# A fused sketch-attention and MLP kernel: the same operations in another order on every engine and in other PSUM banks

## The chip, the cores and the metric

The kernel runs on one core of a Trainium2 chip. The metric is the device time of one execution in microseconds; three runs of the kernel before took 102.84, 103.22 and 104.95 us (median 103.22). A core has five engines that work side by side, each through its own queue in order: TensorE (PE, matrix products into PSUM), VectorE (DVE), ScalarE (ACT), GpSimd (POOL) and SyncE (SP). SP and ACT issue the transfers (DMA) here. An instruction waits until what it reads is written and what it overwrites has been read; whatever stands behind it on its engine waits too.

## What is computed

```python
# attention: q, k, v are (4 batches, 4 heads, 1088 rows, 32); S1, S2 are (8, 32), float64
phi(x): a = x @ S1.T; b = x @ S2.T; return outer(a, b) as 64 features per row
kv  = sum over rows of phi(k)^T v          # (64, 32) per head
z   = sum over rows of phi(k)              # (64,)
x   = (phi(q) @ kv) / (phi(q) @ z + 1e-6)  # heads side by side: (4, 1088, 128)
# block: g_ln (128), w_ch1 (128, 512), w_ch2 (512, 128), the weights float64
xn  = (x - mean) / sqrt(var + 1e-6) * g_ln
out = x + relu(xn @ w_ch1) @ w_ch2         # (4, 1088, 128), float32
```

## The kernel before

Nothing is left to a scheduler. The function defines small named operations (marked `@op`) and a string `PROGRAM` that lists them, with engine letters (`V` VectorE, `A` ScalarE, `G` GpSimd, `S` SyncE) and PSUM bank letters as arguments. The order of the string is the order on each engine's queue. There are eight PSUM banks, `A` to `D`, `M`, `N`, `O`, `K`. A later writer of a bank waits for the readers of what stood there.

The stages, which the string interleaves for the four batches 0 to 3:

- **Loads.** `ld_s`, `ld_g`, `ld_w`, `ld`, `ld_h`, `ld_v`, `ld_vr` fetch the sketches, g, the weights, k and q, and v; `ld_vr` fetches the two last row groups of v in short rows. Constants, masks and pads are made by the `c_` operations; `c_cg` folds g and the mean into a 128x128 matrix.
- **Weights.** The weights come as float64 bit patterns. Operations `w_ex`, `w_bits`, `w_exf`, `w_mant`, `w_low`, `w_e2`, `w_e3`, `w_add` and `w_mul` turn them into float32 by handling exponent, mantissa and low word; index 0 is the sketches, 1 is w_ch1, 2 is w_ch2. `fold` and `fold_cp` multiply w_ch1 by the matrix of `c_cg`.
- **Keys.** `turn_g` and `turn_r` turn k on VectorE; `k_feat` multiplies it by the sketch on PE (L506); `k_tok` turns the features back on VectorE (L516); `k_prod` makes the 64 products per row on GpSimd or VectorE (L82); `k_sum`, `k_zs`, `k_sc` and `k_sccp` make z and put it beside the sketch of q; `k_val` forms kv (L560); `k_vcp`, `k_spr`, `k_rcp` spread it.
- **Queries.** `turn_h`, `turn_r`, `q_feat` (L629), `q_tok` (L639), then `q_ac`, `q_den`, `q_rec` for the denominator, `q_a2` and `q_prod` for the products, `q_turn` (L677), and `num` (L735), which gives x turned, in banks A to D; `num_cp` and `num_r` copy it to SBUF. The first half of batch 0 takes a path of its own: `q_dir` (L595), `q_ac0`, `q_b0`, `q_prod0`, `q_flip`, `q_flcp` and `num0`; `v_flip` and `v_cp` turn v of batch 0 on PE.
- **Block.** x is cut into ten chunks: 0 to 7 of 512 rows, two per batch, and 8 and 9 of 128. `hid` is the first matmul (L843), `relu` its rectifier, `sec` the second matmul for 128 rows (L859). `row_pe`, or `row_turn`, `row_wr` and `row_rd` through DRAM, give x with rows on partitions for the statistics `st_bn`, `st_ag`, `st_pow`; `fin`, or `fin_a` and `fin_g`, scale and add; `store` and `store_r` write out.

`fill` and `bump` are matmuls of ones into bank M whose results nobody reads; they occupy PE where it would wait. The operation around the change that the program's order decides most is a matmul pair such as

```python
    @op
    def hid(z, c, j, t0, t1):
        a, n = P * t0, P * (t1 - t0)
        pe.matmul(banks[z][:, 0:n], w1[:, P * j : P * (j + 1)], cols(c)[:, a : a + n], start=True,
                  stop=True)
```

whose bank `z` must be free and whose columns `cols(c)` must have been copied.

## Time and profile before

| | us |
|---|---|
| profiled execution, its own time | 102.81 |
| its span in the trace | 100.9 |
| PE busy | 95.3 |
| DVE busy | 74.0 |
| POOL busy | 58.4 |
| ACT busy | 41.3 |

The profile is of one execution. The span runs from the first instruction to the last; 1.9 us of the time lie outside it. Busy shares are means over the span. Rows of a timeline start with the start and the length in us, then the engine, the line, the operation and what it writes and reads; a bracket gives idle time of that engine before it and what ended that idle time. Rows of the chain that ended last have start, length and the thing that the end waited for. A float32 matmul counts as two passes in the rows, so that "x2" is one matmul.

### The profile page before, as it was taken

To read this page: it belongs to the slowest core of one execution; us is meant where nothing else is said; L and a number is where in the kernel's file an instruction comes from. 1 tells how busy PE (TensorE), PEld (TensorE's weight loads), DVE (VectorE), ACT (ScalarE), POOL (GpSimd) and SP (SyncE) were. 2 spreads that over 40 slices of the span, in tenths; PEclk is the share of its full clock that TensorE was granted. 3 is DMA by queue.
4 is the path that set the end of the run, shared out by engine and by line. 5 is a ranking of instruction groups with operands and counts; after the bars stand their busy time and mean duration, and the time that the engine had idled before them with its cause. 6 is when DMAs were issued, how large, how long until landed. Compare 5 with 4: busy or idle time off the path is not lost.

```text
span 100.9 us, 3433 instructions
## 1 busy us (share of the span) xinstructions
PE 95.3 (94%) x1355; PEld 68.7 (68%) x1355; DVE 74.0 (73%) x239; ACT 41.3 (41%) x119; POOL 58.4 (58%) x83
## 2 busy tenths in 40 slices
PE   5988999999999999999999999999999999999960
...
PEclk9999999999999999999999999999999999999999
...
GB/s 76 272 293 389 353 370 275 272 218 88 3 6 301 212 164 3 6 130 0 6 107 106 47 59 0 109 153 187 55 107 204 143 122 148 1 115 132 77 119 64
DMA packets 12367, 13.85 MB, mean 137 GB/s; under 512 B 2880, under 2 KB 8768, under 8 KB 12352
## 3 DMA queue, kind: packets, MB, share of 16 engines
...
q14 instruction: 5, 0.04, 0.2%
...
## 4 chain that ended last, share of the span: by engine, by line
PE 78%; DMA 5%; POOL 5%; DVE 2%; ACT 2%; SPq 2%; issue 1%; ACTq 0%; POOLq 0%
PE bankO L859 8%; PE bankM L859 8%; DMA w_raw<-in_moe_w_ch_dram 5%; PE bankN L843 5%; PE bankK L560 5%; PE bankC L843 4%; PE bankK L843 4%; PE bankK L859 4%; PE bankB L843 3%; PE bankA L843 3%; PE bankD L843 3%; PE bankM L250 3%; PE bankA L859 3%; PE bankN L859 3%; POOL ob L888 2%; PE bankA L735 2%
## 5 line engine op out<-in xcount | busy, mean ns | idle before, releaser
L82 POOL TENSOR_TENSOR kp<-kf 128x1024 f32<-128x1024 f32 (+4 forms) x9 | 15.9, 1779 | 0.1
L827 POOL TENSOR_SCALAR va<-mv 128x4 f32<-128x4 f32 (+1 forms) x10 | 2.3, 228 | 18.2 <-DVE mv L822 17.7
L82 POOL TENSOR_TENSOR qp<-a,fq 128x1280 f32<-128x1280 f32 (+1 forms) x5 | 11.1, 2219 | 0.2
L859 PEld LDWEIGHTS bankO<-w,hT 128*128 128x128 f32 x80 | 9.7, 192 | 1.9 <-issue 1.9
L829 POOL TENSOR_TENSOR rstd<-va,mhalf 128x4 f32<-128x4 f32 (+1 forms) x10 | 10.3, 1034 | 0.8
L859 PE MATMUL bankO<-w,hT 128*128 128x128 f32 x80 | 10.4, 277 | 0.0
L859 PEld LDWEIGHTS bankM<-w,hT 128*128 128x128 f32 x72 | 9.0, 192 | 1.9 <-issue 1.9
L677 DVE STREAM_TRANSPOSE qpT<-qp 128x1280 f32<-128x1280 f32 (+1 forms) x7 | 9.6, 1365 | 0.0
L250 PE MATMUL bankM<-ones 128*128 128x256 f32 (+1 forms) x28 | 8.3, 440 | 1.2 <-DVE top L180 1.2
L859 PE MATMUL bankM<-w,hT 128*128 128x128 f32 x72 | 9.3, 275 | 0.0
L816 DVE BATCH_NORM_STATS2 st<-x 128x6 f32<-128x128 f32 x32 | 6.7, 272 | 2.5 <-issue 2.5
L250 PEld LDWEIGHTS bankM<-ones 128*128 128x128 f32 x28 | 5.7, 241 | 2.5 <-DVE top L180 1.2
L851 ACT ACTIVATE hT<-bankC 128x512 f32<-128x512 f32 (+1 forms) x6 | 3.3, 551 | 8.3 <-PE bankB L859 4.7
L843 PE MATMUL bankC<-xT,w 128*128 128x512 f32 x12 | 6.1, 592 | 0.0
L843 PE MATMUL bankN<-xT,w 128*128 128x512 f32 (+1 forms) x14 | 6.1, 516 | 0.0
L851 ACT ACTIVATE hT<-bankN 128x256 f32<-128x256 f32 (+1 forms) x6 | 3.0, 498 | 7.2 <-PE bankN L843 7.2
L82 POOL TENSOR_TENSOR a<-fq,rden 128x160 f32<-128x160 f32 (+1 forms) x6 | 2.8, 463 | 5.2 <-DVE rden L659 4.8
L560 PEld LDWEIGHTS bankK<-kp,vn 128*32 128x32 f32 x288 | 4.2, 110 | 2.3 <-issue 1.1
L851 ACT ACTIVATE hT<-bankK 128x512 f32<-128x512 f32 (+1 forms) x6 | 3.1, 522 | 6.2 <-PE bankK L843 5.3
L457 DVE STREAM_TRANSPOSE qT<-qn 128x512 f32<-128x512 f32 x8 | 5.5, 687 | 0.0
L843 PE MATMUL bankK<-xT,w 128*128 128x512 f32 (+1 forms) x12 | 5.4, 530 | 0.0
L735 PE MATMUL bankD<-qpT,kvr 32*32 32x288 f32 (+1 forms) x64 | 5.2, 386 | 0.0
...
## 6 DMA issues: line engine op xcount, KB each, us to landing
...
```

What stands on the lines that cost most here:

```text
L82: by[eng].tensor_tensor(out=o, in0=a, in1=b, op=ALU.mult)
L250: pe.matmul(M[0][:, 0:w], ones[:, 0:P], ones[:, 0:w], start=True, stop=True)
L457: dve.transpose(_ap(dst[b % 2], 0, P, P * 4 * half, [[32, 4], [P, 4], [1, 32]]), src[b][:, 512 * half : 512 * half + 512],)
L560: pe.matmul(KV[D * h : D * h + D, 0:F], vn[b][:, TW * h + D * u : TW * h + D * (u + 1)], kp[:, H * F * u + F * h : H * F * u + F * (h + 1) ...
L677: dve.transpose(_ap(qpT, 0, P, 32 * u0, [[32, u1 - u0], [TW, 8], [1, 32]]), qp[:, H * F * u0 : H * F * u1])
L735: pe.matmul(X[r][D * h : D * h + D, o : o + w], kvr[b % 2][rows, DM * f + D * h : DM * f + D * h + D], qpT[rows, c : c + w], start=(f == 0 ...
L816: dve.bn_stats(out=sts[slot(c)][:, 6 * t : 6 * t + 6], in_=row_ap(c, t))
L827: pool.tensor_scalar(out=vas[slot(c)][:, 0:n], in0=_ap(mvs[slot(c)], 0, P, 1, [[2, n]]), scalar1=1e-6, scalar2=None, op0=ALU.add)
L829: pool.tensor_tensor(out=rstds[slot(c)][:, 0:n], in0=vas[slot(c)][:, 0:n], in1=mhalf[:, 0:n], op=ALU.pow)
L843: pe.matmul(banks[z][:, 0:n], w1[:, P * j : P * (j + 1)], cols(c)[:, a : a + n], start=True, stop=True)
L851: act.activation(o, i, AF.Relu)
L859: pe.matmul(banks[z][:, DM * t : DM * (t + 1)], h[:, 512 * j + P * t : 512 * j + P * (t + 1)], w2[:, DM * j : DM * (j + 1)], start=(j == 0 ...
```

## The change

Only the string is changed. The same operations stand in another order, and many have another engine letter or another bank; the unused `sk_0` is left out. On loads: both sketches are loaded by ScalarE's queue (`ld_s A`), g by SyncE instead of ScalarE, and all `row_rd` and `row_wr` by SyncE; the short rows of v for batches 1 and 2 come earlier on SyncE, the rest of w_ch1 before k of batch 1. The words of the sketches are worked out on VectorE alone, ahead of the masks. The four turning products of v (`v_flip`) follow each other, in banks M, K, O and C. `fold D` comes after `k_val 0`, and `fold B` replaces `fold M`. The first half of w_ch1 is multiplied on VectorE (`w_mul V 1 0 256`). Of chunk 0 three `hid` come ahead of `q_feat 1`, three `sec` of chunk 0 come ahead of `num 0` and the four of chunk 1 together ahead of `num 1`. `k_val 2` comes just after `num 1`; `q_feat 3` and `k_val 3` come after chunk 3's `hid`, most of `sec 2` and half of `sec 3`.

The start and the part around batch 3's queries in the two strings:

```diff
-ld_w S 1 2 4; c_ones; ld_g A; c_small; c_ac 0; ld_s A 0; ld_s S 1; c_vpad 0; c_kvb; c_vpad 1;
-fill 1 128; ld S k 0 0 16; c_act; c_pads 1; c_pads 0; fill 4 256; c_iota; ld S k 0 16 34;
-c_ac 1; c_m2; c_ident; ld_w S 1 0 2; c_m32; c_m8; ld S k 1 0 34; ld S q 0 16 34;
-w_low A 1 256 512; w_ex V 0 0 32; w_bits V 0 0 32; w_bits V 1 256 512; w_exf A 0 0 32;
-ld_h S q 0 0; w_mant V 1 256 512; w_mant A 0 0 32; w_ex V 1 256 512; ld S v 0 0 32;
-w_e2 V 0 0 32; w_addlow V 0 0 32; w_exf A 1 256 512; w_e3 V 0 0 32; turn_g k 0 0 2;
-ld_vr S 0 1; s_heads G; fill 1 128; w_e2 A 1 256 512; fill 1 128; c_cg V; ld_vr S 0 0; bump 12;
-turn_g k 0 2 4; ld_w S 2 0 4; sk; bump 24; sk_8 A; w_e3 V 1 256 512; sk_q; turn_r k 0;
-ld S q 1 0 34; w_ex V 1 0 256; w_add V 1 256 512; k_feat 0 0 9; w_bits V 1 0 256;
-w_mul G 1 256 512; sk_d; fill 1 256; k_tok 0 0 0 9; sk_b; k_tok 0 1 0 9; sk_qq 0; fill 1 256;
-c_rest; sk_2 A; ld S k 2 0 34; turn_g k 1 0 4; w_mant A 1 0 256; fill 1 256; k_prod G 0 0 3;
-w_exf A 1 0 256; k_sum 0; w_low A 1 0 256; fill 1 128; ld_vr S 1 0; k_zs 0; fill 1 256;
-turn_h q 0 1; k_sc 0; k_prod G 0 5 6; fill 1 256; turn_r q 0; k_sccp F 0; ld_vr S 2 0;
-turn_h q 0 0; k_sccp A 0; q_feat 0 4 9; w_e2 A 1 0 256; k_prod G 0 6 9; turn_r k 1;
-q_dir 0 4 O; q_tok 0 0 4 9; sk_0; q_tok 0 3 4 9; ld_vr S 1 1; q_tok 0 2 4 9; c_vpad 2;
-k_prod G 0 3 5; v_flip 1 K; q_tok 0 1 4 9; q_cp A 0 4 O 16 24; v_flip 2 N; ld_vr S 2 1;
-v_flip 0 D; q_ac0 0 4 O 0; v_flip 3 C; v_cp A 1 K; k_feat 1 0 9; ld_vr S 3 0; v_cp A 0 D;
-q_den 0 0 4; w_e3 V 1 0 256; q_ac G 0 4 9; v_cp A 2 N; v_cp A 3 C; q_rec 0 0 4; fold D 256 512;
-k_tok 1 0 0 9; w_add G 1 0 256; k_val 0; q_b0 0 4 O 0; fold_cp A D 256 512; q_den 0 4 9;
-q_prod0 0 2 O 0; w_mul G 1 0 256; ld S k 3 0 34; q_rec 0 4 9; fill 1 128; f_vcp A;
-w_ex V 2 0 512; q_flip 0 2 1 A; q_a2 G 0 4 9; f_spr C; q_prod0 2 4 O 0; fold M 0 256;
-f_rcp A C; k_vcp A 0; q_prod G 0 4 9; q_flip 0 2 0 D; k_tok 1 1 0 9; ld S q 2 0 34;
-q_flcp A 0 2 1 A; q_flip 2 4 1 O; q_flcp A 0 2 0 D; q_flip 2 4 0 N; turn_h q 1 1;
-fold_cp A M 0 256; k_sum 1; q_flcp A 2 4 1 O; num0 0 2 D; turn_r q 1; q_flcp A 2 4 0 N; k_zs 1;
-turn_h q 1 0; k_sc 1; num0_cp A 0 2 D; num0 2 4 O; ld_v S 1 3; k_sccp V 1; turn_g k 2 0 4;
...
-relu A A 2 0 0 4; q_feat 3 0 9; k_vcp A 2; row_wr A 3; fin_g G 0; k_spr 2; q_tok 3 0 0 9;
-row_rd A 2 3; sec M 2 1; q_tok 3 1 0 9; q_tok 3 2 0 9; k_prod G 3 5 9; hid K 8 1 0 1;
-hid B 3 3 0 4; q_turn 4 9; k_rcp A 2; row_rd S 3 3; row_rd A 3 2; sec M 2 2; row_rd S 3 1;
-relu A B 3 3 0 4; row_rd S 3 0; q_tok 3 3 0 9; k_prod G 3 0 5; hid A 8 2 0 1; row_rd S 2 0;
-q_turn 0 4; hid C 8 0 0 1; hid D 8 3 0 1; hid N 3 1 0 4; st_bn 1; sec M 2 3; relu A N 3 1 0 4;
-st_bn 8; sec M 2 0; hid N 3 2 0 4; relu A D 8 3 0 1; relu V K 8 1 0 1; row_rd A 2 1;
-q_ac V 3 4 9; st_ag 1; relu A C 8 0 0 1; k_val 3; row_rd A 2 2; relu V A 8 2 0 1; st_pow 1;
-relu V N 3 2 0 4; q_den 3 4 9; num 2 0 9; q_rec 3 4 9; k_vcp A 3; fin_a O 1; q_a2 G 3 4 9;
-q_ac G 3 0 4; q_prod G 3 4 9; k_spr 3; num_cp V 2 1 4 8; sec O 3 2; num_cp V 2 3 4 8;
...
+c_ones; ld_s A 1; ld_w S 1 0 2; c_pads 1; ld_s A 0; ld S k 0 0 16; fill 4 256; c_vpad 1;
+c_ident; ld S k 0 16 34; ld_w S 1 2 4; c_ac 0; c_rest; ld S q 0 16 34; c_pads 0; ld S k 1 0 34;
+c_vpad 0; w_bits V 0 0 32; c_kvb; c_small; c_iota; w_ex V 0 0 32; c_act; ld_h S q 0 0;
+w_exf V 0 0 32; w_mant V 0 0 32; w_addlow V 0 0 32; w_bits V 1 0 256; ld S v 0 0 32;
+w_e2 V 0 0 32; w_e3 V 0 0 32; ld_vr S 2 1; s_heads V; fill 1 256; w_ex V 1 0 256;
+turn_g k 0 0 2; ld_vr S 1 0; w_exf A 1 0 256; c_m32; w_e2 A 1 0 256; fill 1 256; c_m2;
+w_mant V 1 0 256; ld_g S; fill 1 128; c_m8; sk; turn_r k 0; turn_g k 0 2 4; fill 1 128; sk_8 A;
+bump 12; ld_vr S 0 1; w_e3 V 1 0 256; k_feat 0 0 9; sk_d; w_ex V 1 256 512; w_bits V 1 256 512;
+sk_b; k_tok 0 0 0 9; fill 1 128; sk_q; ld_vr S 0 0; sk_2 A; bump 24; k_tok 0 1 0 9; sk_qq 0;
+turn_h q 0 1; k_prod G 0 6 9; w_mant A 1 256 512; k_sum 0; w_low A 1 0 256; turn_r q 0;
+fill 1 256; k_zs 0; w_low A 1 256 512; fill 1 128; w_exf A 1 256 512; ld_w S 2 0 4;
+turn_g k 1 0 4; k_sc 0; fill 1 256; k_prod G 0 0 3; w_e2 A 1 256 512; fill 1 128; fill 1 256;
+ld S q 1 0 34; k_sccp F 0; turn_h q 0 0; q_feat 0 4 9; k_sccp A 0; k_prod G 0 5 6; q_dir 0 4 N;
+q_tok 0 3 4 9; k_prod G 0 3 5; q_tok 0 2 4 9; ld S k 2 0 34; q_tok 0 0 4 9; ld S q 2 0 34;
+q_tok 0 1 4 9; v_flip 1 M; turn_r k 1; q_cp A 0 4 N 16 24; c_cg V; w_add G 1 256 512;
+ld_vr S 3 1; v_flip 3 K; q_ac0 0 4 N 0; v_flip 0 O; v_flip 2 C; v_cp A 1 M; ld_v S 1 1;
+k_feat 1 0 9; q_den 0 0 4; v_cp A 3 K; w_e3 V 1 256 512; v_cp A 0 O; ld_vr S 1 1; q_rec 0 0 4;
+v_cp A 2 C; w_mul G 1 256 512; q_b0 0 4 N 0; ld_v S 2 1; k_val 0; k_tok 1 0 0 9; q_ac G 0 4 9;
+q_prod0 0 2 N 0; ld_vr S 2 0; w_add G 1 0 256; fold D 256 512; k_tok 1 1 0 9; f_vcp A;
+k_vcp A 0; w_mul V 1 0 256; q_flip 0 2 0 C; fold_cp A D 256 512; f_spr A; q_prod0 2 4 N 0;
+q_flip 0 2 1 O; q_flcp A 0 2 0 C; ld_v S 1 2; k_sum 1; f_rcp A A; q_flcp A 0 2 1 O;
+fold B 0 256; q_den 0 4 9; w_low A 2 0 512; w_bits V 2 0 512; q_flip 2 4 1 O; k_zs 1;
+q_flip 2 4 0 A; w_ex V 2 0 512; q_flcp A 2 4 1 O; num0 0 2 N; q_rec 0 4 9; ld S k 3 0 34;
+q_flcp A 2 4 0 A; fold_cp V B 0 256; q_a2 G 0 4 9; k_sc 1; num0_cp A 0 2 N; turn_h q 1 0;
+k_spr 0; c_ac 1; w_mant A 2 0 512; num0 2 4 O; q_prod G 0 4 9; turn_h q 1 1; hid C 0 1 0 2;
+w_exf A 2 0 512; ld_v S 1 0; k_sccp V 1; hid M 0 3 0 2; turn_r q 1; ld_v S 1 3; turn_g k 2 0 4;
+relu A C 0 1 0 2; hid N 0 0 0 2; relu A M 0 3 0 2; q_feat 1 0 9; num0_cp A 2 4 O; ld_v S 2 0;
+w_e2 A 2 0 512; w_add G 2 0 512; ld_v S 2 3; hid O 0 1 2 4; q_tok 1 1 0 9; hid K 0 3 2 4;
+q_tok 1 3 0 9; hid M 0 2 0 2; w_e3 V 2 0 512; k_rcp A 0; hid B 0 2 2 4; relu A O 0 1 2 4;
+relu A M 0 2 0 2; q_tok 1 0 0 9; hid D 0 0 2 4; w_mul G 2 0 512; relu A B 0 2 2 4; turn_r k 2;
+turn_r q 2; row_pe 0 M; relu A N 0 0 0 2; q_tok 1 2 0 9; relu A K 0 3 2 4; k_feat 2 0 9;
+relu A D 0 0 2 4; turn_h q 2 1; row_cp A 0 M; c_vpad 3; q_ac G 1 0 4; sec O 0 2; k_tok 2 0 0 9;
+q_ac G 1 4 9; sk_qq 2; q_den 1 4 9; k_prod G 1 0 5; k_tok 2 1 0 9; sec O 0 0; q_turn 4 9;
...
+row_rd S 3 2; sec N 3 1; row_rd S 2 3; q_turn 0 4; store S 0 1 0 4; k_spr 2; q_feat 3 0 9;
+k_val 3; q_tok 3 0 0 9; q_tok 3 1 0 9; q_tok 3 2 0 9; sec N 3 3; k_rcp A 2; q_tok 3 3 0 9;
+k_vcp A 3; q_ac G 3 0 4; k_spr 3; num 2 0 9; q_den 3 0 4; k_rcp A 3; q_ac V 3 4 9; q_den 3 4 9;
+q_rec 3 0 4; q_rec 3 4 9; q_a2 G 3 0 4; st_bn 8; sec O 2 1; q_a2 G 3 4 9; num_cp A 2 1 0 4;
+num_cp V 2 3 0 4; num_cp A 2 1 4 8; num_cp V 2 2 0 4; num_cp A 2 0 4 8; q_prod G 3 0 4;
+num_cp A 2 0 0 4; num_cp V 2 3 4 8; st_ag 8; sec N 3 0; num_cp V 2 2 4 8; num_r V 2; st_bn 3;
+hid K 4 1 0 4; row_turn 4; q_prod G 3 4 9; hid A 4 0 0 4; relu A K 4 1 0 4; st_bn 2;
+row_wr S 4; hid D 4 2 0 4; row_turn 5; relu A A 4 0 0 4; st_ag 2; row_wr S 5; sec M 8 0;
+q_turn 0 4; relu A D 4 2 0 4; st_pow 2; hid B 5 1 0 4; row_rd S 4 3; q_turn 4 9; st_pow 8;
+fin_a O 2; hid D 4 3 0 4; row_rd S 5 2; hid A 5 3 0 4; relu V B 5 1 0 4; row_rd S 4 2;
```

102 lines of the change are left out of this document (46 added, 56 removed).

## The prediction

> **What bounds the kernel now.** I read the page first, for the busy shares and the forty slices.
>
> ```profile
> span 100.9 us, 3433 instructions
> ...
> PE 95.3 (94%) x1355; PEld 68.7 (68%) x1355; DVE 74.0 (73%) x239; ACT 41.3 (41%) x119; POOL 58.4 (58%) x83
> ...
> PE   5988999999999999999999999999999999999960
> ...
> PEclk9999999999999999999999999999999999999999
> ```
>
> TensorE is busy in every slice but the first few and the last, at a granted clock of 9 tenths or more throughout. A busy share can hide waits, so I went to the chain that ended last, where each step on PE has its start and length.
>
> ```profile
> 12.13 0.25 PE bankA L629
> ...
> 25.49 0.43 PE bankK L843 x2
> ...
> 27.77 0.63 PE bankN L843 x2
> ...
> 31.86 0.86 PE bankK L843 x2
> ...
> 34.46 1.14 PE bankK L560 x72
> ...
> 36.91 0.89 PE bankM L859 x8
> ...
> 40.63 0.38 PE bankA L735 x4
> ...
> 42.16 1.09 PE bankO L859 x8
> ...
> 49.69 0.35 PE bankA L629
> ...
> 74.93 0.49 PE bankD L843 x2
> ...
> 96.47 0.91 PE bankA L859 x8
> ...
> 97.40 0.35 DVE ob L872
> ```
>
> These are unit prices: a `hid` of 512 columns 0.86 us, of 256 columns 0.43, a `sec` 0.89, a `k_val` 1.14, a `num` about 1.5 (40.63 to 42.16). From the first real query work (`q_feat 0`, the L629 row at 12.1) PE runs almost without a hole to 97.4; one `fin` and the last stores follow. So the time is: the start up to `q_feat 0` (12.1 us), the PE work after it, the holes in that work, and a tail of 3.5 us (97.4 to 100.9). Work is the same in both kernels; fills (dummy matmuls) only occupy waiting time. A new order can therefore win only holes and start, and can lose without limit.
>
> How large are the holes? I add unit prices. From `q_feat 0` to the last half `hid` of chunk 0 (end 27.77 + 0.43 = 28.2): eight half `hid` 3.44, eight flips 0.88, two folds 0.86, `num0` 1.2, `q_dir` 1.05, `k_val` 1.14, `num 0` 1.1, `q_feat` twice 1.15, `k_feat` twice 1.3, `v_flip` 0.7, `row_pe` 0.43, the small sums and turns 1.45: 14.7 us of work in 16.1, so 1.4 us of holes. From 28.2 to 97.4: 34 `sec` 30.3, 28 full `hid` 24.1, 8 small 1.7, three `k_val` 3.4, three `num` 4.5, the rest 4.0: 68.0 us in 69.2, so 1.2 us of holes. (The smaller prices are estimates from start-to-start distances in the same view.) At most 2.6 us can be won after 12.1.
>
> **The change, part by part.** *The start.* Rows of VectorE and PE in the timeline:
>
> ```profile
> 2.46 0.24 DVE L207 TENSOR_TENSOR m<-bit,head 128x2 f32<-128x2 int32 x1
> ...
> 2.82 0.24 DVE L207 TENSOR_TENSOR m<-bit,head 128x4 f32<-128x4 int32 x1
> ...
> 3.72 0.17 DVE L277 TENSOR_SCALAR ex<-s_raw 16x32 uint32<-16x32 uint32 x1 [0.38 <-DMA s_raw<-in_S_dram]
> ...
> 4.97 0.71 DVE L434 STREAM_TRANSPOSE kT<-kn 128x512 f32<-128x512 f32 x1
> 5.60 0.25 DVE L355 TENSOR_SCALAR cg<-ident,g_raw 128x128 f32<-128x128 f32 x1
> ...
> 7.08 0.40 PE L506 MATMUL bankA<-kT,sk 64*32 64x288 f32 x1 [0.28 <-DVE kT L452]
> ...
> 7.83 0.29 DVE L277 TENSOR_SCALAR ex<-w_raw 128x256 uint32<-128x256 uint32 x1 [0.90 <-DMA w_raw<-in_moe_w_ch_dram]
> ...
> 8.71 0.47 DVE L516 STREAM_TRANSPOSE kf<-bankA 128x288 f32<-128x288 f32 x1
> ...
> 11.66 0.19 DVE L553 TENSOR_REDUCE skq<-bankK 128x8 f32<-128x32 f32 x1
> ```
>
> Before, VectorE makes its masks while the sketches load (0.36 each), and stops 0.90 at the second half of w1 with the turning of k's features (8.71) behind it. After, the sketch words are first in its queue, so the three masks (1.1 us) follow the sketches' arrival, taken at 3.72 again: both loads now issue from ScalarE, 0.72 and 1.17, and 1.17 is also the later one's issue before. From 3.72: seven small word operations at 0.1 and one of 256 columns, 4.8; `s_heads` and `w_ex` 5.2; turning half of k (0.63, from 4.97 to 5.60) 5.85; masks and `w_mant` 7.15; the rest of k 8.0. `k_feat 0` starts at 8.05 instead of 7.08. But the stop at 7.83 is gone, as w1's second half is issued one place earlier on SP and wanted at 8.4: `w_e3`, `sk_d` and two word operations end at 8.85, and `k_tok 0` starts at 8.87 against 8.71. Two of the three query turns now come ahead of k 1's turn, so that `k_sccp` runs at about 11.75 against 11.66. Start: +0.1 us, hidden or not, taken as nothing. If the sketches land later, all of this moves one for one.
>
> *The loads on SyncE.* g moves from ScalarE's first place to the eleventh on SP.
>
> ```profile
> 5.09 1.66 SPq L127 DMA_DIRECT2D vn<-in_v_dram  x2
> ...
> vn<-in_v_dram SPq DMA_DIRECT2D x8, 16.0 KB, 6.5
> ```
>
> The short rows of v, of which two now stand ahead of g and four ahead of w2, cost the queue 1.66 us a pair at worst and land in a median of 6.5 us. With g issued at 5.3 to 6.9 it lands by 13.4 at the latest; `c_cg` stands on VectorE at about 14. Nothing, with 0.6 us of cover; without it, `q_ac0` and all behind it wait.
>
> *From 12 to 26 us.* Prices:
>
> ```profile
> 15.05 0.70 PE L360 MATMUL bankD<-w1g,cg 128*128 128x256 f32 x2
> ...
> 17.72 2.40 POOL L82 TENSOR_TENSOR qp<-a,fq 128x1280 f32<-128x1280 f32 x1
> ...
> 18.43 0.38 ACT L77 COPY v<-bankA 128x256 f32<-128x256 f32 x1
> 18.70 0.39 ACT L77 COPY v<-bankD 128x256 f32<-128x256 f32 x1
> ...
> 21.10 0.72 ACT L288 ACTIVATE exf<-ex,m 128x512 f32<-128x512 uint32 x1
> ...
> 21.86 0.72 ACT L310 ACTIVATE exf<-exf,m 128x512 f32<-128x512 f32 x1
> ...
> 26.76 1.78 POOL L323 TENSOR_TENSOR mant<-mant,low 128x512 f32<-128x512 f32 x1 [1.22 <-DVE qT L452]
> ...
> 28.62 1.27 POOL L82 TENSOR_TENSOR w<-mant,bits 128x512 f32<-128x512 f32 x1
> ```
>
> `fold D` filled the wait for v's copies at 15.05; now `k_val 0` waits for them itself (to 15.7, a loss of 0.5) and `fold D` follows. One fill of 128 columns is gone (0.2). After that three `hid` stand ahead of `q_feat 1`, where before PE waited for `num0` copies and VectorE's query turns; `sec 0` starts only when w2 is ready. I walked the queues at the prices above. VectorE: both `q_prod0` done by 18.4, w2's first words by 19.4, `q_rec` 19.55. ScalarE: the copies of flips and folds by 20.3 (0.27 a copy), w2's `w_mant` and `w_exf` (0.75 each) by 21.8, two `relu` and a copy 22.55, `w_e2` 24.05, `k_rcp` and six `relu` 25.9. GpSimd: `q_a2`, then `q_prod` 2.40 to 22.4, `w_add` 1.78 to 24.2, `w_mul` 1.27 to 25.95. PE: three `hid` done 21.95, `q_feat 1` 22.65, five `hid` 24.8, `row_pe` 25.3, `k_feat 2` 26.0. Before, the same set without `num 0` and `k_sum 2` would have ended at 28.2 - 1.4 = 26.8. I take 26.1: a gain of 0.7.
>
> `w_mul V 1 0 256` and `fold_cp V B` add 0.7 us to VectorE here and take 1.1 off GpSimd and ScalarE; they stand ahead of `q_prod0 2 4` and the query turns, and are in the walk. `w_mant` for w2 goes the other way.
>
> *From 26 us on.* PE has work for each moment if three things hold: `num 0` waits for `q_turn 4 9` (VectorE, done 28.8) while three `sec` and `k_sum 2` cover to 28.95; all four `sec 0` and `sec 1` come before `num 1`; `k_val 2` fills the wait for `num 1`'s copies. At the end PE no longer waits here:
>
> ```profile
> 74.93 0.30 PEld L843 LDWEIGHTS bankD<-xTr,w 128*128 128x128 f32 x2 [0.31 <-ACT xT L77]
> ```
>
> Two `sec` (1.78 us) now cover those copies: a gain of 0.3 to 0.4. The tail is the same in kind; `st_pow 9` now ends about when `sec C 9 0` does, at no cost.
>
> Sum: start 0, middle -0.7, later -0.4: -1.1 on 102.81 us (span 100.9 plus 1.9 around it), 101.7. Handoffs that my walk sets at nothing took 0.1 to 0.3 us each in the rows with a releaser; I give 0.2 back: **101.9 us**. The three runs shown have a median of 103.22, 0.4 above the profiled execution, so the ratio may read -0.9% or -1.3%.
>
> **The rivals.** *Nearly all holes close* (faster by over 2%). All of 2.6 us, less some 0.2, gives 100.4. For it: the new order has its fillers at each copy I looked at. Against it: `k_val 0`'s wait is new.
>
> *ScalarE becomes the bound from 17 to 26 us* (slower). Its queue there has no idle time: I counted copies at the 0.27 between the starts of 18.43 and 18.70, while one lasts 0.38. If dependent ones do not overlap, the stretch sums to 10.9 us and not 8.9, `relu` and `w_e2` come 2.0 later, with `w_e3`, `w_mul` and `sec 0` behind them. It decides once ScalarE is 1.1 us later than walked; at 2.0 the time is 103.8, and with GpSimd's 1.27 then alone on the path 105.1.
>
> *Batch 3's features come too late.* `q_feat 3` ran at 49.7, 22 us before `num 3`; now only some 13.5 us of PE work lie between. Through `q_tok`, `q_prod`, `st_pow 2` and `fin_a O 2` the chain frees bank O at about 69.2, when `hid O 5 2` wants it at 69.7.
>
> ```profile
> 40.36 2.65 POOL L82 TENSOR_TENSOR kp<-kf 128x1024 f32<-128x1024 f32 x1
> ...
> 51.05 1.94 POOL L82 TENSOR_TENSOR kp<-kf 128x1024 f32<-128x1024 f32 x1
> ```
>
> If GpSimd's products take 2.65 instead of 1.94, two of them cost 1.5, less 0.5 of cover: 102.9. With another 1.3 for a norm in front, 104.2.
>
> *PE's pace falls at the start.* PE has nothing from its last fill (about 6.2) to 8.05.
>
> ```profile
> 2.18 1.06 PE L250 MATMUL bankM<-ones 128*128 128x256 f32 x2
> ...
> 2.61 1.06 PE L250 MATMUL bankM<-ones 128*128 128x256 f32 x2
> ```
>
> Early passes of 256 columns start 0.43 apart, though the granted clock reads full there; later two such passes take 0.43 (25.49). If the slow pace returns for `k_feat`, `k_sum` and `k_sc`, 1.1 us doubles: 103.0. [...]
>
> *The order changes nothing that counts*: other holes take the place of those closed, 102.8.
>
> **How the numbers follow.** Forecast (101.2 to 102.6) 0.30; nearly all holes 0.25; ScalarE 0.14; batch 3 0.09; pace 0.04; nothing 0.06; a stall in a queue that I did not walk, of 3 us or more, 0.12. Over 2% faster (2.06 us, about what a measurement of this kernel can tell from no change) is below 101.15: the second case and the lower edge of the first, 0.29. Over 2% slower is above 105.3 on the median, 104.9 on the profiled execution: half of ScalarE and of batch 3 at their far ends, and the stall, 0.24. The rest 0.47. The range leaves about a tenth out on each side: 100.1 to 105.0.
>
> **What would show it.** Right: `k_feat 0` near 8, `k_tok 0` near 8.9 with no wait on w1, `q_feat 0` near 12.1, the first `sec` near 26.1 with GpSimd's `w_mul` ending just before, `num 3` ending near 72.9, PE idle for less than 1.5 us after 12. Wrong: `q_feat 0` after 13, ScalarE busy without idle past 27, PE waiting for `fin_a O 2` near 70, or a stop of `c_cg` on g.

## The result and the profile after

The kernel after took 103.98 us (median of 6 runs, 103.68 to 104.70) against 103.25 us for the kernel before in the same comparison (6 runs): a ratio of 1.011, 95% interval 1.007 to 1.015. This ratio and those below are of the fast runs alone: more than a third of all runs of the kernel before, two of these six (104.66 and 104.95), were some 1.4 us slower than its others and are left out. The forecast was 101.9 us. The profiled execution took 103.68 us, with a span of 101.9 us against 100.9. From the page of after: the span, the busy times, and the granted clock in forty slices.

```profile
span 101.9 us, 3428 instructions
...
PE 95.7 (94%) x1355; PEld 69.2 (68%) x1355; DVE 74.0 (73%) x239; ACT 41.2 (40%) x119; POOL 57.5 (56%) x82
...
PEclk9999999999999999999999999999999999999999
```

Busy times (within 1 us) and clock are those of before; the page alone doesn't tell where the microsecond went. The timeline of after does, in the start (start, length, engine, line, what is written and read; in the bracket the idle time ahead of it and what ended it).

```profile
3.86 0.17 DVE L282 TENSOR_SCALAR bits<-s_raw 16x32 uint32<-16x32 uint32 x1 [2.75 <-DMA s_raw<-in_S_dram]
...
6.26 0.12 DVE L206 TENSOR_SCALAR bit<-row 128x4 int32<-128x4 int32 x1
...
7.24 0.42 ACT L410 ACTIVATE sk<-bankK,m 128x16 f32<-128x16 f32 x2
...
7.71 0.43 PE L506 MATMUL bankA<-kT,sk 64*32 64x288 f32 x1 [0.86 <-ACT sk L410]
...
9.03 0.48 DVE L516 STREAM_TRANSPOSE kf<-bankA 128x288 f32<-128x288 f32 x1
...
10.79 0.19 DVE L539 TENSOR_TENSOR zT<-bankK,m 128x32 f32<-128x32 f32 x1 [0.19 <-ACT mant L296]
...
12.05 0.15 DVE L553 TENSOR_REDUCE skq<-bankK 128x8 f32<-128x32 f32 x1
...
14.61 0.70 DVE L355 TENSOR_SCALAR cg<-ident,g_raw 128x128 f32<-128x128 f32 x1
...
97.03 1.06 PE L859 MATMUL bankC<-w,hT 128*128 128x128 f32 x8
```

VectorE waits 2.75 us for the sketches, and makes the masks from 6.26 on, when work is waiting. `skq` is there at 12.20 (12.05 + 0.15); it starts 0.39 us later than in the kernel before (11.66). The chain that ended last shows what PE did then, and the later places that the prediction named (start, length, what the end waited for):

```profile
11.54 0.14 PE bankK L545 x2
11.68 1.17 PE bankM L250 x6
12.85 0.25 PE bankA L629
...
15.29 0.66 ACT vn L77 x2
15.96 0.14 issue
16.09 1.38 PE bankK L560 x72
17.48 0.63 PE bankD L360 x2
...
27.59 2.88 PE bankO L859 x24
...
46.11 1.05 PE bankM L843 x2
...
63.55 1.09 PE bankO L859 x8
...
74.83 1.09 PE bankK L859 x8
```

Three fills (L250) fill PE's queue to 12.85, although `skq` was ready at 12.20. In the kernel before, one fill stood there; its chain and its first and last rows on PE of the same kind are:

```profile
11.62 0.51 PE bankM L250 x2
```
```profile
12.06 0.32 PE L629 MATMUL bankA<-qT,skq 32*32 32x160 f32 x1
...
96.30 1.06 PE L859 MATMUL bankA<-w,hT 128*128 128x128 f32 x8
```

So before ran from its first query product at 12.06 to its last matmul's end at 97.36 (96.30 + 1.06), 85.30 us. After ran from 12.78 (the timeline's first start of L629) to 98.09, 85.31 us. In these two profiles the whole loss on PE, 0.72 us, lies ahead of `q_feat 0`: 0.39 us until `skq`, 0.33 us in PE's queue behind it. Behind `q_feat 0` the new order is worth nothing. The rest, 0.3 us, comes behind the last matmul: 3.5 us to the span's end before, 3.8 after.

### The profile page after: what moved, and what is told of

Its sections match the earlier page's. It is cut to its first block, busy times and chain, and to the rows that moved or that the text cites. A ratio compares the mean times of both kernels' runs of the same rounds, so it can differ in the third digit from the quotient of the medians.

```text
span 101.9 us, 3428 instructions
## 1 busy us (share of the span) xinstructions
PE 95.7 (94%) x1355; PEld 69.2 (68%) x1355; DVE 74.0 (73%) x239; ACT 41.2 (40%) x119; POOL 57.5 (56%) x82
## 4 chain that ended last, share of the span: by engine, by line
PE 83%; DVE 6%; DMA 2%; POOL 1%; ACT 1%; issue 1%; POOLq 1%; ACTq 1%; DVEq 0%
PE bankO L859 8%; PE bankN L859 7%; PE bankA L843 7%; PE bankD L843 5%; PE bankK L560 5%; PE bankM L843 5%; PE bankK L859 4%; PE bankA L735 3%; PE bankC L843 3%; PE bankA L859 3%; DVE ob L872 3%; PE bankK L843 3%; PE bankO L843 3%; PE bankM L250 2%; DMA s_raw<-in_S_dram 2%; PE bankN L843 2%
## 5 line engine op out<-in xcount | busy, mean ns | idle before, releaser
L859 PE MATMUL bankN<-w,hT 128*128 128x128 f32 x72 | 9.0, 276 | 0.0
L250 PE MATMUL bankM<-ones 128*128 128x256 f32 (+1 forms) x28 | 7.8, 424 | 1.2 <-DVE ones L173 1.2
L859 PEld LDWEIGHTS bankN<-w,hT 128*128 128x128 f32 x72 | 8.4, 192 | 0.1
L843 PE MATMUL bankA<-xT,w 128*128 128x512 f32 x16 | 8.2, 593 | 0.0
L250 PEld LDWEIGHTS bankM<-ones 128*128 128x128 f32 x28 | 5.9, 230 | 2.1 <-DVE ones L173 1.2
L888 POOL TENSOR_TENSOR ob<-ob,x 128x512 f32<-128x512 f32 x4 | 5.1, 1276 | 3.0 <-ACT ob L878 3.0
L859 PEld LDWEIGHTS bankK<-w,hT 128*128 128x128 f32 x40 | 4.9, 192 | 1.2 <-issue 1.2
L843 PE MATMUL bankD<-xT,w 128*128 128x512 f32 (+1 forms) x12 | 5.7, 557 | 0.0
L82 POOL TENSOR_TENSOR a<-fq,rden 128x128 f32<-128x128 f32 (+1 forms) x5 | 2.1, 429 | 6.1 <-DVE rden L659 5.6
L843 PE MATMUL bankM<-xT,w 128*128 128x512 f32 (+1 forms) x12 | 5.4, 530 | 0.0
L859 PE MATMUL bankK<-w,hT 128*128 128x128 f32 x40 | 5.4, 277 | 0.0
L560 PE MATMUL bankK<-kp,vn 128*32 128x64 f32 x288 | 5.0, 220 | 0.3 <-ACT vn L77 0.3
```

What stands on the lines that cost most here:

```text
L82: by[eng].tensor_tensor(out=o, in0=a, in1=b, op=ALU.mult)
L250: pe.matmul(M[0][:, 0:w], ones[:, 0:P], ones[:, 0:w], start=True, stop=True)
L560: pe.matmul(KV[D * h : D * h + D, 0:F], vn[b][:, TW * h + D * u : TW * h + D * (u + 1)], kp[:, H * F * u + F * h : H * F * u + F * (h + 1) ...
L859: pe.matmul(banks[z][:, DM * t : DM * (t + 1)], h[:, 512 * j + P * t : 512 * j + P * (t + 1)], w2[:, DM * j : DM * (j + 1)], start=(j == 0 ...
L888: by[eng].tensor_tensor(out=o, in0=o, in1=i, op=ALU.add)
```

## The experiments

Two theories stood against each other. **The start is paid in full**: whatever delays `q_feat 0` delays the end by as much. **The middle sets the time**: the copies of v, `c_cg` and `fold D` between 14 and 18 us decide. The table has every run: ratio to the kernel before with its interval, then from each timeline the start of `q_feat 0`, the end of the last matmul and the time between, in us.

| run | ratio | q_feat 0 | last matmul | between |
|---|---|---|---|---|
| before | 1 | 12.06 | 97.36 | 85.30 |
| after | 1.011 (1.007 to 1.015) | 12.78 | 98.09 | 85.31 |
| two_fills | 1.0055 (1.0032 to 1.0077) | 12.16 | 97.57 | 85.41 |
| before_fills | 1.0083 (1.0038 to 1.0128) | 12.68 | 98.06 | 85.38 |
| masks_first | 1.0015 (0.9992 to 1.0037) | 12.09 | 97.50 | 85.41 |
| start_before | 1.0053 (1.0015 to 1.0092) | 12.39 | 97.75 | 85.36 |
| sec_cover | 0.9961 (0.9924 to 0.9998) | 12.24 | 98.40 | 86.16 |
| tail | 0.9987 (0.9950 to 1.0025) | 12.20 | 97.61 | 85.41 |
| best1 | 1.0448 (1.0373 to 1.0524) | 15.18 | 102.09 | 86.91 |
| best2 | 1.0459 (1.0394 to 1.0524) | 15.21 | 102.44 | 87.23 |
| cg_early | 1.0032 (1.0005 to 1.0058) | 12.30 | 98.91 | 86.61 |
| flips_first | 1.0129 (1.0092 to 1.0167) | 12.32 | 98.86 | 86.54 |
| best3 | 1.0104 (1.0050 to 1.0159) | 11.79 | 98.76 | 86.97 |
| no_fills | 110.39 us against 103.33 | 14.04 | 103.96 | 89.92 |
| one_fill_less | 1.0059 (1.0026 to 1.0093) | 12.61 | 98.21 | 85.60 |
| sk_sooner | 1.0062 (1.0029 to 1.0095) | 12.60 | 98.01 | 85.41 |
| best5 | 1.0024 (0.9989 to 1.0060) | 11.28 | 97.47 | 86.19 |
| e3_sooner | 0.9951 (0.9908 to 0.9994) | 11.62 | 97.04 | 85.42 |
| best6 | 0.9946 (0.9902 to 0.9991) | 11.56 | 97.30 | 85.74 |

The profiled executions of sec_cover and cg_early hold one stop of PE of about 1.2 us (last section), that of best6 a shorter one; their ratios say more than their last two columns. The row of no_fills has the medians of all runs; five of its six took 108.58 to 110.65 us, one 142.75.

### The fills on PE

two_fills, on the kernel after:

```diff
-turn_g k 1 0 4; k_sc 0; fill 1 256; k_prod G 0 0 3; w_e2 A 1 256 512; fill 1 128; fill 1 256;
+turn_g k 1 0 4; k_sc 0; fill 1 256; k_prod G 0 0 3; w_e2 A 1 256 512;
```

> The kernel after without the last two fills (128 and 256 columns) between k_sc 0 and q_feat 0. Theory 1, the start is paid in full: q_feat 0 starts about 0.15 us after skq is done on VectorE (12.05 + 0.15), so near 12.4 in place of 12.85, and since PE has no idle time behind it, everything later moves by the same 0.4 to 0.5 us: k_val 0 near 15.65, last matmul near 97.7, the time about 0.65 us above the kernel before (ratio near 1.006, after it was 1.011). Rival, the stretch from 14 to 18 us sets the time (c_cg and the copies of v ahead of k_val 0, fold D no longer a cover): q_feat 0 comes earlier but k_val 0 stays near 16.1 and the ratio near 1.011.

Measured: half of the loss is gone (1.011 to 1.0055). Its timeline, first query product and last matmul:

```profile
12.16 0.32 PE L629 MATMUL bankB<-qT,skq 32*32 32x160 f32 x1
...
96.51 1.06 PE L859 MATMUL bankC<-w,hT 128*128 128x128 f32 x8
```

`q_feat 0` came 0.62 us earlier than in after, the last matmul 0.52. In this execution the sketches also came 0.20 us earlier (3.66 against 3.86), so the fills account for some 0.4 us of it. The rival falls: `k_val 0` moved along, to 15.57. The counterpart, before_fills, puts the same two fills into the kernel before:

```diff
-turn_h q 0 1; k_sc 0; k_prod G 0 5 6; fill 1 256; turn_r q 0; k_sccp F 0; ld_vr S 2 0;
+turn_h q 0 1; k_sc 0; k_prod G 0 5 6; fill 1 256; fill 1 128; fill 1 256; turn_r q 0; k_sccp F 0;
```

> The kernel before with two more fills (128 and 256 columns) between k_sc 0 and q_feat 0, which is what the kernel after has there. Theory 1 (PE works through its queue in order, and what a fill takes beyond the wait that it covers is paid in full): the three fills end near 12.4, q_feat 0 starts 0.4 us later, near 12.5, and the time is 0.4 us above the kernel before (ratio near 1.004). Rival (a fill takes no time on PE that other work could have used): no change.

The chain and the timeline of before_fills:

```profile
11.58 1.17 PE bankM L250 x6
```
```profile
11.62 0.19 DVE L553 TENSOR_REDUCE skq<-bankK 128x8 f32<-128x32 f32 x1
...
12.68 0.32 PE L629 MATMUL bankA<-qT,skq 32*32 32x160 f32 x1
```

`skq` is ready at 11.81 and waits for PE's queue until 12.68. The last matmul ends 0.70 us later than before; 85.38 us lie between. The theory holds; I had put the price at 0.4 us; it is 0.6 at `q_feat 0` and 0.8% in the timed runs.

### The masks on VectorE

masks_first is two_fills with the constants and masks back in the wait for the sketches (`c_m8`, behind `ld_g S`, moves along and isn't shown):

```diff
-ld_s A 1; ld_w S 1 0 2; c_pads 1;
+ld_s A 1; ld_w S 1 0 2; c_iota; c_pads 1;
...
-c_vpad 0; w_bits V 0 0 32; c_kvb; c_small; c_iota; w_ex V 0 0 32; c_act;
+c_vpad 0; c_small; c_act; c_m32; c_m2; c_m8; w_bits V 0 0 32; c_kvb; w_ex V 0 0 32;
...
-turn_g k 0 0 2; ld_vr S 1 0; w_exf A 1 0 256; c_m32; w_e2 A 1 0 256; fill 1 256; c_m2;
+turn_g k 0 0 2; ld_vr S 1 0; w_exf A 1 0 256; w_e2 A 1 0 256; fill 1 256;
```

> The kernel after without those two fills and with the constants and the three masks ahead of the sketch words on VectorE (the numbers of the heads first on GpSimd), as before the change. Theory 1: the 1.1 us of VectorE work then lie in the wait for the sketches; k_feat 0 near 7.1 to 7.3 instead of 7.71, skq near 11.4 to 11.6, q_feat 0 near 11.7, last matmul near 97.0, the time 0.1 us above to 0.3 us below the kernel before. Rival 1 (the stretch from 14 to 18 us sets the time): no better than the kernel without the two fills. Rival 2 (another chain sets skq, the sketch's copies s2b on ScalarE and zT): k_feat 0 comes earlier, skq hardly, and half of the gain is lost.

Another 0.4 us are gone (1.0055 to 1.0015), the loss as a whole within the interval. In the one profile it hardly shows:

```profile
2.59 0.16 DVE L207 TENSOR_TENSOR m<-bit,head 128x4 f32<-128x4 int32 x1
...
4.12 0.17 DVE L282 TENSOR_SCALAR bits<-s_raw 16x32 uint32<-16x32 uint32 x1 [1.37 <-DMA s_raw<-in_S_dram]
...
6.51 0.39 PE L374 MATMUL bankK<-ident,s_f 16*128 16x16 f32 x2
```

The masks are done at 2.75, but in this execution the sketches came 0.46 us later than in that of two_fills (3.66), and the sketch product (L374) stood behind fills until 6.51, with its input ready at 5.69. Single profiles of the start differ by half a microsecond; only the medians of many runs tell such edits apart (103.27 us for two_fills, 102.86 for masks_first).

### The order behind the start, and the late wait

start_before has the order of before up to `q_feat 0` and `k_sccp`, and the rest in the order and banks of after. sec_cover is the kernel before with one `sec` moved:

```diff
-hid D 9 0 0 1; row_rd S 4 2;
+sec K 5 3; hid D 9 0 0 1; row_rd S 4 2;
...
-row_wr A 7; row_cp V 9 N; sec K 5 3; row_turn 6;
+row_wr A 7; row_cp V 9 N; row_turn 6;
```

> The order of the kernel before up to q_feat 0, and from there the order and banks of the kernel after. Theory 1 (only the start was lost, and the rest of the new order is worth nothing or little): q_feat 0 at 12.1, k_val 0 near 15.4, last matmul near 97.3, the time within 0.3 us of the kernel before. Rival, the new order behind q_feat 0 costs time itself (the lost cover of k_val 0): 0.5 us or more above the kernel before. The prediction's own step (the new order behind q_feat 0 wins 1.1 us): 0.8 to 1.1 us below the kernel before.

> The kernel before with one sec of chunk 5 moved ahead of chunk 9's four hid, so that it covers the copies of num 3 at 74.93. If the 0.31 us in the weight loads' row there are a hole that an order can close, as the prediction took it: 0.3 us below the kernel before (ratio near 0.997). Rival, such gaps are part of what PE's work takes when one kind of matmul follows another, and there was hardly any hole in the order before: 0 to 0.1 us.

With the start of before, the new order was not faster, so the 1.1 us that I had forecast for it don't exist. Its ratio, 1.0053, even reaches the 0.5 us that the rival named; by the medians (103.30 us, and 102.96 for the runs of before that count) it is 0.3%. Its profile doesn't put this loss in the middle: 85.36 us on PE are those of before, `q_feat 0` came 0.33 us later with the same order ahead of it, as the sketches landed 0.38 us later (first word at 4.10, against 3.72), and 3.8 us follow the last matmul. Whether the other runs lost in the same places isn't shown.

sec_cover won 0.4% by itself, though its interval all but reaches 1. Its trace agrees: from the start of the first `sec` behind `num 3` to that of the last `sec` it took 22.26 us (75.08 to 97.34), before 22.65 (73.65 to 96.30), 0.39 less for the same work. So the wait at 74.93 was real and could be covered. The new order covers it too, and gives as much back elsewhere between 12 and 74 us; no run here shows where. What can be read is that a `sec` behind a `num` takes 1.09 us and a `hid` behind a `k_val` 1.05 (rows 63.55 and 46.11 above), against 0.89 and 0.86 within a row of their kind.

tail is masks_first with `st_ag 7`, `st_pow 7` and the three `st_` of chunk 9 right after `st_pow 6`. The early norms of chunk 7 overwrite those that chunk 5's last sum still reads; no instruction is left out here or in best1 and best2, which share the edit.

> The kernel after without the two fills, with the masks first, and with the statistics of chunks 7 and 9 (st_ag 7, st_pow 7, st_bn 9, st_ag 9, st_pow 9) right after st_pow 6. Theory 1: from the last matmul to the end of the span it took 3.54 us in the order before and 3.81 in the order after, since the last norm on GpSimd ends at 98.20 (last matmul 98.09) and seven stores are issued from 97.6 on; with the norms early this falls to 3.55, the time 0.25 us less than with the masks first alone, 0.1 us below the kernel before. Rival: the last store's own landing sets it, 3.8 us stay, no gain.

The last `fin` now came 0.09 us after the last matmul (0.15 in after), yet 3.8 us still passed to the span's end. The ratio is 0.3% below that of masks_first, within the intervals. By the trace the norms were not the cause; what makes the last stores 0.2 us slower stays open.

### Starts that ran into something else

best1 and best2 build on tail and change VectorE's order and PE's fills at once (shown for best1, operations of other engines left out; best2 drops two more fills ahead of `sk`, and moves `w_e2` behind `sk_8` and `w_e3` behind `k_sccp`):

```diff
-turn_r q 0; fill 1 256; k_zs 0; fill 1 128; turn_g k 1 0 4; k_sc 0; fill 1 256; k_sccp F 0; turn_h q 0 0;
+turn_r q 0; k_zs 0; turn_h q 0 0; fill 1 128; k_sc 0; fill 1 256; k_sccp F 0; q_feat 0 4 9; k_sccp A 0; turn_g k 1 0 4;
...
-k_tok 0 1 0 9; sk_qq 0;
+k_tok 0 1 0 9; c_cg V; sk_qq 0;
```

> As the run with the early norms, and in the start: the turning of k 1 (1.23 us on VectorE) behind k_sccp instead of ahead of it, the last turning of q ahead of k_sccp, one fill of 256 columns less ahead of k_zs, and c_cg right after k_tok 0 in place of between q_tok and q_ac0. Theory 1 (q_feat 0 sets all that follows): skq near 11.3, q_feat 0 near 11.6 in place of 12.1, the last matmul 0.5 us earlier. Theory 2 (from q_feat 0 to the flips VectorE's chain through q_tok, q_ac0, q_den, q_b0 and q_prod0 sets the pace, 4.85 us in both orders, and the moved turning is only put into it): 0.1 us from the start, but 0.7 us from c_cg, which took 0.70 us in that chain. Together by theory 2 the flips start 0.5 to 0.8 us earlier. The time 0.5 to 0.8 us below the kernel before (ratio 0.992 to 0.995); if it is not below 0.998, PE's work behind 18 us was not dense.

> As the run before it in this call, with two fills less ahead of the first sketch product (256 and 128 columns), the copy of the sketch on ScalarE ahead of w_e2, and w_e3 of w1's first half behind k_sccp. Theory 1 (PE and ScalarE queues ahead of k_feat 0 cost up to 0.5 us, as the sketch product stood behind fills until 7.0 in the run without the two fills, with s_f ready at 5.3): k_feat 0 near 7.5 instead of 7.9, q_feat 0 0.3 us earlier, time 0.3 us less than the run before it. Rival (with fewer fills PE is still at its slow pace of 0.43 us a pass of 256 columns when k_feat 0 comes): k_feat, k_sum and k_sc take up to 1 us longer, and nothing is won or up to 0.7 us lost.

Both lost over 4%, for a reason that I had not written down: where g is loaded. Timeline of best1:

```profile
12.06 0.66 DVE L355 TENSOR_SCALAR cg<-ident,g_raw 128x128 f32<-128x128 f32 x1 [2.48 <-DMA g_raw<-in_moe_g_ln_dram]
...
13.60 0.63 PE L545 MATMUL bankK<-zT,s2b 128*128 128x32 f32 x2 [2.79 <-DVE zT L539]
...
15.94 2.02 PE L595 MATMUL bankN<-skd,qT 128*128 128x96 f32 x8
```

On SyncE's queue g lands only at 12.0; VectorE stood still for it, PE for 2.79 us, and after that PE ran at half pace: `q_dir` (L595) took 2.02 us, against 1.06 in after (13.33 to 14.39 in its chain). best2 waits for g in the same way, but its pace has another reason, the one that its rival names. Timeline of best2:

```profile
9.18 0.80 PE L250 MATMUL bankM<-ones 128*128 128x128 f32 x2
...
15.98 2.02 PE L595 MATMUL bankN<-skd,qT 128*128 128x96 f32 x8
...
20.24 1.58 PE L560 MATMUL bankK<-kp,vn 128*32 128x64 f32 x72
```

The same fill took 0.49 us in best1 (8.96). With fewer fills PE was slow ahead of its wait already, and still at `k_val 0` (1.58 us, against 1.38 in after). cg_early repeats the one edit with g loaded by ScalarE behind the sketches, on masks_first:

```diff
-ld_s A 0; ld S k 0 0 16; fill 4 256;
+ld_s A 0; ld_g A; ld S k 0 0 16; fill 4 256;
...
-w_mant V 1 0 256; ld_g S; fill 1 128;
+w_mant V 1 0 256; fill 1 128;
...
-k_tok 0 1 0 9; sk_qq 0;
+k_tok 0 1 0 9; c_cg V; sk_qq 0;
...
-q_cp A 0 4 N 16 24; c_cg V; w_add G 1 256 512;
+q_cp A 0 4 N 16 24; w_add G 1 256 512;
```

> The kernel after without the two fills and with the masks first; besides, g is loaded by ScalarE right behind the sketches and c_cg stands right after k_tok 0 1, where VectorE waits 0.2 us for k_sum anyway. With g on SyncE it landed 6.0 us after its issue, at 12.0, and c_cg that early made VectorE stop for 2.5 us (the runs best1 and best2); on ScalarE it took 2.9 us in the order before, so it lands near 5. Theory 1 (behind q_feat 0 PE is dense but for the wait of k_val 0 for the copies of v): c_cg's 0.70 us on VectorE between q_tok and q_ac0 are off the path, and the time stays that of the masks first (ratio to the kernel before 1.000 to 1.002). Theory 2 (VectorE's chain from q_tok to q_prod0 sets the flips): 0.4 to 0.7 us less, ratio near 0.996.

`c_cg` took 0.25 us at 9.79, without a wait, and the ratio was 1.0032 against 1.0015 for masks_first: no gain from taking it out of the middle. The run alone doesn't settle it, as `skq` came 0.21 us later there (12.00 against 11.79). But the one row of after in which PE waits behind 12.8 us names ScalarE's copy of v, and none names VectorE; its chain there was not the bound.

no_fills is masks_first without the eight fills and the `bump` of 12 ahead of `k_feat 0` (the first and the last of the places are shown):

```diff
-c_pads 1; ld_s A 0; ld S k 0 0 16; fill 4 256; c_vpad 1;
+c_pads 1; ld_s A 0; ld S k 0 0 16; c_vpad 1;
...
-fill 1 128; sk_8 A; bump 12; ld_vr S 0 1;
+sk_8 A; ld_vr S 0 1;
```

> The kernel after without the two fills and with the masks first, and without any fill ahead of k_feat 0. The rows of all orders so far show passes of 256 columns 0.43 us apart in the first microseconds of fills and 0.215 apart from about 5 to 6 us on. Theory 1 of the prediction's rival (PE starts slow and needs some microseconds of work before it runs at its full pace): k_feat 0 starts earlier, near 7.5, but takes 1 us instead of 0.6, and k_sum, k_sc and the fills between them run at half pace too; the time rises by 0.5 to 1.5 us over the run with the masks first. Rival (the slow pace belongs to the first microseconds of the execution, whatever PE does): 0 to 0.3 us less.

The median was 110.4 us. Timeline of no_fills:

```profile
11.39 1.65 PE L250 MATMUL bankM<-ones 128*128 128x256 f32 x4
...
20.68 1.28 PE L560 MATMUL bankK<-kp,vn 128*32 128x64 f32 x36 [2.50 <-issue]
```

Passes of 256 columns were still 0.43 us apart at 11.4 us. The fills do buy the pace, and the rival falls. `q_feat 0` came at 14.04, 1.95 us later than in masks_first. Not all 7 us are this pace: 2.5 us are a stop inside `k_val 0` with no releaser (last section), and behind it the granted clock read 0.82 (18 to 22 us) and 0.75 (22 to 26 us), against 1.00 from 5 to 18 us.

flips_first put v's turning products and copies ahead of `q_dir`, best3 changed the start as well (the operations' old places and the bank letters that follow from `q_dir`'s and `fold`'s new banks are left out):

```diff
-q_feat 0 4 9; k_sccp A 0; k_prod G 0 5 6; q_dir 0 4 N; q_tok 0 3 4 9;
+q_feat 0 4 9; v_flip 1 M; v_flip 3 K; v_flip 0 O; v_flip 2 N; k_sccp A 0; v_cp A 1 M; v_cp A 3 K; v_cp A 0 O; v_cp A 2 N; k_prod G 0 5 6; q_dir 0 4 D; q_tok 0 3 4 9;
```

> As the run with c_cg early, and the four turning products of v and their copies right behind q_feat 0, ahead of q_dir, which goes to bank D, with fold D in bank M. If the wait of k_val 0 for v's copies (0.33 us in the row, 0.4 to 0.5 with the slower start of its 72 passes) is the one hole left in this stretch: k_val 0 starts 0.4 us earlier, near 15.1, and the time falls by 0.4 us, ratio near 0.996 where c_cg early alone stays at 1.000. Rival (GpSimd's products kp and w1g, ready near 15 and 16.5, are the next to wait for): 0 to 0.2 us.

> As the run before it in this call, and the turning of k 1 behind k_sccp, the last turning of q ahead of it, one fill of 256 columns less ahead of k_zs, w_e2 of w1's second half behind the copy of skq, and the statistics of chunk 9 after st_pow 6. Theory 1 (each us of q_feat 0 is a us at the end): skq near 11.3 and q_feat 0 near 11.6 in place of 12.1, time 0.4 to 0.5 us less than the run before it, ratio near 0.992. Rival (VectorE, which has 1.2 us more behind q_feat 0, or v's landing near 11.6 then sets k_val 0): q_feat 0 as early, but nothing at the end.

In both, `skd` is copied after `v_flip 3 K` has overwritten its bank, and `q_dir` overwrites bank D ahead of the turning of the query features there. So VectorE waits for `q_dir`; timeline of flips_first:

```profile
14.96 0.35 DVE L639 STREAM_TRANSPOSE fq<-bankD 128x160 f32<-128x160 f32 x1 [2.17 <-PE bankD L595]
```

`k_val 0` started at 17.04. The runs don't answer whether v's copies are the one hole there.

### What else held the start back

one_fill_less, sk_sooner and best5 take up the sketch product that waits behind fills: one_fill_less drops the fill ahead of `w_mant`, sk_sooner keeps all fills and moves the product, best5 joins this with the other edits of the start. All three also move `w_e2` and `w_e3`. sk_sooner, on masks_first:

```diff
-w_exf A 1 0 256; w_e2 A 1 0 256; fill 1 256; w_mant V 1 0 256; ld_g S; fill 1 128; sk; turn_r k 0;
+w_exf A 1 0 256; sk; fill 1 256; w_mant V 1 0 256; ld_g S; fill 1 128; turn_r k 0;
...
-sk_8 A; bump 12; ld_vr S 0 1; w_e3 V 1 0 256; k_feat 0 0 9;
+sk_8 A; w_e2 A 1 0 256; bump 12; ld_vr S 0 1; k_feat 0 0 9;
...
-turn_r q 0; fill 1 256; k_zs 0;
+turn_r q 0; w_e3 V 1 0 256; fill 1 256; k_zs 0;
```

> As the run with the masks first, with one fill of 256 columns less ahead of the sketch product, the copy of the sketch (ScalarE) ahead of w_e2, and w_e3 of w1's first half on VectorE ahead of k_zs. Theory 1 (fills in PE's queue hold the sketch product back, and the start is paid in full): the sketch product at 5.8 to 6.5 in place of 6.5 to 7.0, k_feat 0 at 7.4 to 7.6, q_feat 0 0.3 us earlier, the time 0.2 to 0.4 us less than with the masks first (ratio to the kernel before 0.998 to 1.000). Rival (the fills are needed for the pace): after less than 5 us of unbroken work PE stays at 0.43 us a pass, k_feat 0 takes 0.9 us or more in place of 0.6 and the time rises by 0.5 us or more.

> As the run before it in this call, but no fill is left out; the sketch product stands ahead of the last 384 columns of fills instead of behind them. Theory 1: sketch product at 5.7, k_feat 0 at 7.5, with as many fills, so the pace turns before k_feat 0: time 0.3 to 0.5 us less than with the masks first (ratio 0.997 to 0.999). Rival 1: the fills now stand between the sketch product and k_feat 0 and hold k_feat 0 back until 7.9 as before: no gain. Rival 2: a gap of some tenths of a us ahead of the sketch product keeps PE at the slow pace: 0.5 us or more lost.

> As the run before it in this call, with g loaded by ScalarE and c_cg behind k_tok 0, the turning of k 1 behind k_sccp, the last turning of q ahead of it, a fill of 256 columns less ahead of k_zs, w_e2 of w1's second half behind the copy of skq, and the statistics of chunk 9 after st_pow 6. Theory 1: q_feat 0 at 11.3 to 11.6, and 85.4 us from there to the last matmul as in all orders so far: last matmul near 96.9, ratio 0.991 to 0.995. Rival (VectorE, which has 1.6 us more behind q_feat 0, then sets the flips): q_feat 0 as early, but 0.3 us or more are given back by 18 us, seen as more than 85.7 us from q_feat 0 to the last matmul.

`k_feat 0` did come at 7.6 (7.08 in best5), and yet none of the three gained. Timelines of one_fill_less and of best5:

```profile
9.35 1.51 POOL L82 TENSOR_TENSOR kp<-kf 128x768 f32<-128x768 f32 x1 [0.22 <-DVE kf L516]
...
9.90 1.23 DVE L318 SCALAR_TENSOR_TENSOR bits<-w_raw,ex 128x256 uint32<-128x256 uint32 x1
...
12.31 0.15 DVE L553 TENSOR_REDUCE skq<-bankK 128x8 f32<-128x32 f32 x1
```
```profile
10.99 1.61 DVE L318 SCALAR_TENSOR_TENSOR bits<-w_raw,ex 128x256 uint32<-128x256 uint32 x1
```

`w_e3`, which I had moved without a thought, takes 0.38 us in after (8.08, ahead of GpSimd's first product) and 1.23 or 1.61 here, beside that product. e3_sooner and best6 move this one operation of sk_sooner and best5 to the 0.4 us in which VectorE waits for `k_feat 0`:

```diff
-sk_b; k_tok 0 0 0 9;
+sk_b; w_e3 V 1 0 256; k_tok 0 0 0 9;
...
-turn_r q 0; w_e3 V 1 0 256; fill 1 256; k_zs 0;
+turn_r q 0; fill 1 256; k_zs 0;
```

> As the run with the sketch product sooner, but w_e3 of w1's first half stands right ahead of k_tok 0, where VectorE waited 0.39 us and GpSimd is idle. Theory 1 (VectorE's w_e3 was held up by GpSimd's product, and the start is paid in full): w_e3 0.38 us long, k_tok 0 still at 8.4, zT near 10.2 in place of 11.05, skq near 11.45, q_feat 0 near 11.8 in place of 12.6; the time 0.7 us less than with the sketch product sooner, ratio to the kernel before 0.998 to 1.000. Rival (w_e3 is slow by itself, 1.2 us, or the time isn't set by the start): ratio stays near 1.006.

> The combined kernel (sketch product sooner, g loaded by ScalarE, c_cg behind k_tok 0, the turning of k 1 behind k_sccp) with w_e3 of w1's first half right ahead of k_tok 0. Theory 1: q_feat 0 at 11.3 as there, but VectorE turns k 1 from 11.0 to 12.2 and the query features from 12.2 in place of 13.7, so that k_val 0 and the flips come near 15.0 and 16.7 (15.5 and 17.2 there) and the last matmul is near 96.9; ratio 0.993 to 0.997. Rival (another chain, GpSimd's products or v's copies, holds k_val 0 at 15.5): ratio near 1.002 as there.

Timeline of e3_sooner:

```profile
5.81 0.36 PE L374 MATMUL bankK<-ident,s_f 16*128 16x16 f32 x2 [0.46 <-DVE s_f L82]
...
7.84 0.41 DVE L318 SCALAR_TENSOR_TENSOR bits<-w_raw,ex 128x256 uint32<-128x256 uint32 x1
...
11.62 0.29 PE L629 MATMUL bankA<-qT,skq 32*32 32x160 f32 x1 [0.17 <-DVE skq L553]
...
95.98 1.06 PE L859 MATMUL bankC<-w,hT 128*128 128x128 f32 x8
```

`q_feat 0` at 11.62, the last matmul at 97.04, 85.42 us between, and 0.9951 of the kernel before. One operation, moved into a wait, was worth 1.1% by the ratios (1.0062 to 0.9951): 0.98 us at `q_feat 0`, 0.97 at the end. e3_sooner and best6 beat both kernels, the two alike within their intervals. How much they win over the kernel before is less sure: the runs of before that count in this comparison spread from 102.66 to 104.11 us, and the medians, 102.66 for e3_sooner and 102.80 for best6 against 102.89, differ by 0.2% and 0.1% only. best6 started its queries hardly earlier than e3_sooner (11.56 against 11.62). best5 gave 0.8 us of its start back, as its rival said: VectorE has the turning of k 1 behind `q_feat 0` there.

## Why the prediction was wrong

**The start** ("+0.1 us, hidden or not, taken as nothing") is the step that failed. It cost 0.72 us in the profiles. VectorE was walked: `k_feat 0` at 7.71 (8.05), `k_tok 0` at 9.03 (8.87), `skq` at 12.05 (11.75). This last row is 0.39 us later than in before, where I had 0.09; the other 0.33 us are PE's own queue, which was not walked. The prediction says that fills "only occupy waiting time"; three of them stood where one had, 0.66 us longer (1.17 against 0.51), and PE takes its queue in order. Removing two of them won 0.5%, adding two to before lost 0.83%, and the masks, which I did count and set beside other work, cost another 0.4%. The second step that failed is the gain of 1.1 us behind the start: none of it came (next three points). Of the 1.8 us between 101.9 and the profiled 103.68, some 0.7 are the start, 0.9 the missing gain (1.1 less the 0.2 given back) and 0.3 the tail (rounded, and from single profiles).

**The holes.** I took 85.3 us less a sum of unit prices, 82.7, for 2.6 us of holes. After shows one wait of 0.33 us on PE behind 12.8 (ahead of `k_val 0`) and still needs 85.31 us. The prices were too small at changes of kind, as far as rows show them: 1.09 and 1.05 against 0.89 and 0.86. The prediction's own rows had this: it priced the last half `hid` at 0.43, and its row (27.77) says 0.63. A remainder of 3% between two large sums was then error for the most part, though no run splits it up; one hole was shown, at 74.93, worth 0.4%.

**From 12 to 26 us** (gain 0.7): no gain. The first `sec` came at 27.59, 14.8 us after `q_feat 0`, against 14.0 in the walk and 14.9 for the same set before (it ended at 28.40, not 28.2, less 1.4). `k_val 0`'s wait was seen, and put a little high: `k_val 0` came 3.3 us after `q_feat 0` (16.09), where the forecast has 3.6 (15.7).

**Later** (gain 0.4): the wait at 74.93 is gone, and by itself it is worth what I said (sec_cover). Net of the rest behind 27.6 us it came to nothing.

**The loads.** `c_cg` didn't stop for g, as said; the landing at 12.0 left 2.6 us and not 0.6. But `c_cg` took 0.70 us in its new place, against 0.25 in the row of before.

**The tail** ("at no cost"): 0.3 us. **The rivals**: ScalarE was busy almost without a stop up to 27.8 us (past 27 was the sign named; 0.7 us of it is the later start) and then idle for 4.0 us, but no row of PE behind `k_val 0` waits for it. `hid O 5 2` at 71.6 waited for nothing, and the pace at the start was full from `k_feat 0` on, behind a wait of 0.86 us (0.40 to 0.43 us a product of 288 columns, as in before; 0.66 to 0.69 in no_fills). The 0.04 that I gave a fall of the pace was an estimate of mine, from no run. None of the three set the time. "Nothing that counts" was the nearest, 0.9 us too fast by its 102.8 on the profiled execution's scale; it had nothing to say of the start.
